# A gated mix of two spectral filters: frequency groups as the outer loop, rows turned from SBUF to SBUF, and one joint inverse

## Chip, cores, metric

One core of a Trainium2 chip. The metric is the device time of one execution in microseconds (us); results were compared with the reference. PE is TensorE, DVE is VectorE, ACT is ScalarE, POOL is GpSimd; SP is the engine that does nothing but issue DMAs here.

## The reference

```python
def _A_ref(x, w_r, w_i):                      # _B_ref is the same with B's filter
    X = jnp.fft.rfft2(x.astype(jnp.float32), axes=(-2, -1))   # x: 1 x 2048 x 1024
    X = X * (w_r + 1j * w_i)                                  # filter: 2048 x 513
    return jnp.fft.irfft2(X, s=(S, D), axes=(-2, -1)).astype(jnp.bfloat16)

g = sigmoid((A_x * gate_w).sum(-1, keepdims=True))            # one gate per row
return g * _A_ref(A_x, A_w_r, A_w_i) + (1 - g) * _B_ref(A_x, B_w_r, B_w_i)
```

The input is transformed once and multiplied by two filters of 2048 x 513 complex numbers; two inverse transforms are mixed by a gate for each row. Inputs and output are bf16, and the transforms are matrix products with fixed matrices: 2048 = 128 (n1) x 16 (n2) along the rows, 1024 along d with real and imaginary parts folded.

## The kernel before

It works on 16 groups `kg` of 128 row frequencies. `stage_d` transforms along d, `stage_s2` does the second step of the row transform, `prod` multiplies by a filter on DVE (two groups at once), and `stage_i1` starts the inverse with the *data* as the stationary matrix, so that its result comes out turned; the eviction scatters it with a stride of 128 elements. Then comes an inverse over d for each branch and each row group `n2`, and a last stage that mixes both branches.

```python
    def wload(b):                                  # a filter: 18 DMAs, mostly 256 rows of 1026 B each
        for pm in range(2):
            for ii in range(4):
                for c in range(2):
                    ...
                    if pm == 0:
                        part(16 * ii, 1, 0, 16)
                    elif ii < 3:
                        part(80 + 16 * ii, -1, 0, 16)
                    ...
        dma("sp", prs, [], [("W", b)] + ...)        # one event for the whole filter

    def stage_i1(b, kg):
        for lb in range(4):
            for c in range(2):
                w = ap(RING, p + c * 512 + lb % 2 * 256 + lb // 2, [[2, 128]])      # data is stationary
                fns.append(mm(pslot(s, lb * 256, [[1, 256]]), w, ap(KI, z + c * 256, [[1, 256]]), c == 0, c == 1))
        ...
        ev(1024, ap(VR[b], kg * 8, [[128, 128], [1, 8]]), pslot(s, 0, [[8, 128], [1, 8]]), [("ps", s)], w)

    def stage_dinv(b, n2):                         # inverse over d, once for each branch
        ...
    def s1inv(n2):                                 # n1 inverse, mixes A and B through RA and RB
        ...
    for t in range(16 + LAG):
        ...                                        # rest of stage_i1(1, .), gmix, stage_dinv(0, .)
    for t in range(17):
        if t < 16:
            stage_dinv(1, t)
        if t >= 1:
            s1inv(t - 1)
```

Of the kernel before, what the change touches and what calls it, by code (L numbers as in the profile page):

```python
# [4 lines left out]
dt = mybir.dt  # L5
ACT = mybir.ActivationFunctionType
ALU = mybir.AluOpType
AP = bass.AP
BF = dt.bfloat16

NS = 514
PW = 128
# [7 lines left out]

def make_consts():

# [5 lines left out]
    kord = (np.arange(16)[:, None] + 16 * np.arange(4)[None, :]).reshape(-1)  # L28
    k1 = kord[None, None, :]
# [5 lines left out]
    C["F"] = F.reshape(128, 2048)  # L35
# [5 lines left out]
    C["RM"] = R.reshape(128, 2048)  # L41
# [3 lines left out]
    for h in range(2):  # L45
        d = (h * 128 + np.arange(128))[:, None] + 0.5
        lev, lod = 2 * m, 2 * m + 1
        les = np.where(m == 0, 512, 2 * m)
        DM[:, 0, h] = np.cos(pi2 * lev * d / 1024)
        DM[:, 1, h] = -np.sin(pi2 * lod * d / 1024)  # L50
        DM[:, 2, h] = -np.sin(pi2 * les * d / 1024)
        DM[:, 3, h] = np.cos(pi2 * lod * d / 1024)
# [4 lines left out]
    for par in range(2):  # L57
        for h in range(2):
            l = (2 * (h * 128 + np.arange(128)) + par)[:, None]
            DI[:, par, h, 0] = np.where(l == 0, 1.0, 2.0) / 1024 * np.cos(pi2 * l * d / 1024)  # L60
            li = np.where(l == 0, 512, l)
            DI[:, par, h, 1] = -np.where(li == 512, 1.0, 2.0) / 1024 * np.sin(pi2 * li * d / 1024)
# [3 lines left out]
    KI = np.zeros((2, 2, 128, 2, 16, 4, 2))  # L66
    for z in range(2):
        for pm in range(2):
            for k2 in range(16):
                for ii in range(4):  # L70
                    i = ii if pm == 0 else 3 - ii
                    po = k2 * 8 + pm * 4 + ii
                    spec = (z == 1 and i == 0)
                    for q2 in range(16):
# [16 lines left out]
                        K = KI[z, :, po, :, q2, i, :]  # L91
# [11 lines left out]
    C["KI"] = KI.reshape(2, 2, 128, 256).transpose(2, 0, 1, 3).reshape(128, 1024)  # L103
    gs = np.full((64, 2), 8.0)
    gs[:, 1] = -8.0
    gs[0] = 4.0
    C["GS"] = np.repeat(gs.reshape(128, 1), 16, axis=1)
    one = np.zeros((128, 2))
    one[0] = 1.0
    C["ONE"] = one  # L110
    idt = np.zeros((128, 16))
    idt[:16] = np.eye(16)
    C["ID"] = idt
    return C


class Op:
    __slots__ = ("eng", "idx", "fns", "deps", "raw", "dma", "clock", "need", "count", "waits", "pos")

    def __init__(self, eng, idx, fns, dma, pos):  # L120
        self.eng, self.idx, self.fns, self.dma, self.pos = eng, idx, fns, dma, pos
        self.deps, self.raw = set(), set()
        self.need = False
        self.count = 0


class Sched:


    ENG = ("pe", "act", "dve", "pool", "sp")  # L130

    def __init__(self):
        self.q = {e: [] for e in self.ENG}
        self.all = []
        self.writer, self.readers = {}, {}

    def op(self, eng, fns, reads=(), writes=(), dma=False):
        if not isinstance(fns, (list, tuple)):
            fns = [fns]
        o = Op(eng, len(self.q[eng]), list(fns), dma, len(self.all))  # L140
        self.q[eng].append(o)
        self.all.append(o)
        for k in reads:
            assert k in self.writer, k
            o.deps |= self.writer[k]
            o.raw |= self.writer[k]
        for k in writes:
            o.deps |= self.writer.get(k, set())
            o.deps |= self.readers.get(k, set())
        for k in reads:  # L150
            self.readers.setdefault(k, set()).add(o)
        for k in writes:
            self.writer[k] = {o}
            self.readers[k] = set()
        o.deps.discard(o)
        return o

    def solve(self):
        known = {e: {} for e in self.ENG}

        def merge(kn, c):
            for k, v in c.items():
                if v > kn.get(k, -1):
                    kn[k] = v
        for o in self.all:
            kn = known[o.eng]
            o.waits = []
            for d in sorted(o.deps, key=lambda d: -d.pos):
                if d.dma:
                    if d in kn:  # L170
                        continue
                    kn[d] = 1
                else:
                    if d.eng == o.eng == "pe":
                        continue
                    if kn.get(d.eng, -1) >= d.idx:
                        continue
                    d.need = True
                o.waits.append(d)
                merge(kn, d.clock)  # L180
# [3 lines left out]
        for e in self.ENG:  # L184
# [5 lines left out]
    def emit(self, nc):  # L190
        self.solve()
        sems = {e: nc.alloc_semaphore("s_" + e) for e in self.ENG}
        dsem = {o: nc.alloc_semaphore(f"s_d{i}") for i, o in enumerate(o for o in self.all if o.dma)}

        def run(e, name):
            for o in self.q[name]:
                for d in o.waits:
                    if d.dma:
                        e.wait_ge(dsem[d], 16 * len(d.fns))
                    else:  # L200
                        e.wait_ge(sems[d.eng], d.count)
                for f in o.fns:
                    ins = f(e)
                    if o.dma:
                        ins.then_inc(dsem[o], 16)
                if o.need:
                    ins.then_inc(sems[name], 1)
            if name == "sp":
                for o in self.all:
                    if o.dma == "out":  # L210
                        e.wait_ge(dsem[o], 16 * len(o.fns))
# [22 lines left out]

def bass_gated_mix__spectral_gfnet__spectral_gfnet__prompt_kernel(
    nc, A_x, A_w_r, A_w_i, B_x, B_w_r, B_w_i, gate_w, out
):
    C = make_consts()
# [11 lines left out]
    R1 = sb("R1", 16384)  # L250
    R2 = sb("R2", 32 * NS)
    R3 = sb("R3", 16384)
    R4 = sb("R4", 16384)
    R5 = sb("R5", 32 * NS)
    FM = sb("FM", 2048)
# [3 lines left out]
    DI = sb("DI", 2048)  # L259
    RM = sb("RM", 2048)  # L260
    GS = sb("GS", 16)
    ONE = sb("ONE", 2)
    ID = sb("ID", 16)
    V6 = sb("V6", 256)
    RING = sb("RING", 11264)
    GROW = sb("GROW", 512)
    X5 = sb("X5", 32)
    P5 = sb("P5", 192)
    V5 = sb("V5", 256)
    ZG = sb("ZG", 16)  # L270
    G8 = sb("G8", 8)
# [3 lines left out]
    S = Sched()  # L275
# [4 lines left out]
    WR = {0: R5, 1: R2}  # L280


    load = {"act": 0.0, "dve": 0.0}
    slot_n = [0]
    nslots = [3]

    def slot():
        s = slot_n[0] % nslots[0]
        slot_n[0] += 1
        return s  # L290

    def dve(ns, fns, reads, writes):
        load["dve"] += ns
        return S.op("dve", fns, reads, writes)

    def ev(n, outap, inap, reads, writes, eng=None, bias=0.0):
        ca, cd = 170 + 0.833 * n, 150 + 1.04 * n
        if eng is None:
            eng = "act" if load["act"] + ca <= load["dve"] + cd + bias else "dve"
        load[eng] += ca if eng == "act" else cd  # L300
        if eng == "act":
            S.op("act", lambda e: e.activation(outap, inap, ACT.Copy), reads, writes)  # L302
        else:
            S.op("dve", lambda e: e.tensor_copy(outap, inap), reads, writes)  # L304

    def pslot(s, off, dims, p0=0, np_=128):
        return ap(PS, s * 1024 + off, dims, p0, np_)

    def misc(b, off, dims, np_=128):
        return ap(PS, b * 512 + off, dims, 0, np_)  # L310
# [7 lines left out]
    def dma(eng, pairs, reads, writes, kind=True):  # L318
        S.op(eng, [lambda e, d=d, s=s: e.dma_start(d, s) for d, s in pairs], reads, writes, dma=kind)  # L319

    def cload(eng, t, key, n):
        dma(eng, [(ap(t, 0, [[1, n]]).bitcast(dt.uint16), cst[key].ap())], [], [key])


    def xload(a, b):
        dma("sp", [(ap(R1, a * 1024, [[1024, b - a], [1, 1024]]), xv[:, a:b, :])], [], [("x", i) for i in range(a, b)])

    xload(0, 2)
    cload("sp", FM, "F", 2048)
    dma("act", [(ap(R2, 2048, [[1, 1024]], 0, 1), gate_w.rearrange("(o d) -> o d", o=1))], [], ["gw"])  # L330
    cload("act", ONE, "ONE", 2)
    for a, b in ((2, 4), (4, 8), (8, 12), (12, 16)):
        xload(a, b)
    cload("sp", DM, "DM", 2048)
    cload("sp", S2, "S2", 768)
    cload("sp", KI, "KI", 1024)
    cload("sp", GS, "GS", 16)
    cload("sp", ID, "ID", 16)

    def wload(b):  # L340

        prs = []
        T = WR[b]
        P = pit[id(T)]
        for pm in range(2):
            for ii in range(4):
                for c in range(2):
                    src = wsrc[b][c]
                    n = src.shape[-1]

                    def part(r0, step, k0, k1):
                        prs.append((AP(T, (4 * pm + ii) * P + (2 * k0 + c) * NS, [[8 * P, 16], [2 * NS, k1 - k0], [1, n]]),
                                    AP(src.tensor, src.offset + r0 * n, [[128 * n, 16], [step * n, k1 - k0], [1, n]])))
                    if pm == 0:
                        part(16 * ii, 1, 0, 16)
                    elif ii < 3:
                        part(80 + 16 * ii, -1, 0, 16)
                    else:
                        part(127, -1, 1, 16)
                        part(64, 1, 0, 1)  # L360
        dma("sp", prs, [], [("W", b)] + (["zrow", "gwt"] if b else []))
    wload(0)
# [283 lines left out]
```

## Time and profile before

| | before |
|---|---|
| time, median of 2 runs | 162.69 us (162.27 to 163.12) |
| span of the profiled execution | 159.0 us |
| mean granted clock of TensorE | 0.968 |
| busy: PE, DVE, ACT | 78%, 76%, 77% |
| last stage | 123 to 159, 36 us |

Two more views matter later. The first is the page's throughput line: 40 slices of the span, GB/s in each. The filters (8.4 MB) pass in slices 5 to 17 at about 170 GB/s, and then there is hardly any transfer until the output.

```profile
GB/s 168 296 429 415 257 168 167 177 167 165 179 168 170 181 169 169 197 191 4 0 0 0 0 5 0 0 0 4 0 0 1 4 112 152 86 180 123 145 132 132
```

The timeline of SP's queue gives start in us, duration, what is issued. SP issued these four filter loads after it had issued nothing for 1.7 us (32.45 to 34.19):

```profile
34.19 0.57 SPq L319 DMA_DIRECT2D R<-in_B_w_r_dram  x1
34.81 0.64 SPq L319 DMA_DIRECT2D R<-in_B_w_i_dram  x1
35.48 0.65 SPq L319 DMA_DIRECT2D R<-in_B_w_r_dram  x1
36.17 0.65 SPq L319 DMA_DIRECT2D R<-in_B_w_i_dram  x1
```

A filter load that nothing holds back keeps SP for about 0.6 us. Other issues of this kernel, of constants, show 0.42 to 0.58. Most of the filter loads of 256 KB show about 1.4 us, because there the DMA engines set the pace; so the 0.6 us of the issue itself cost nothing here.

### The profile page before, as it was taken

Reading aid. Unit: us, or ns where it says so; the run is one execution under the profiler, and the core shown is the slowest. Engines: PE = TensorE matmul, PEld = TensorE weight load, DVE = VectorE, ACT = ScalarE, POOL = GpSimd, SP = SyncE. Lnnn points to the kernel's source line nnn. Section 1 sums busy time; section 2 is a strip of 40 time slices with the busy share of each in tenths; the row PEclk is TensorE's granted clock in tenths of the full one; section 3 lists DMA queues with packets and bytes.
Section 4 is the critical chain, followed back from the end, with each engine's and each line's share of the span. In section 5 each row is a group of like instructions: output and inputs, shape, how many; then the busy total and the mean of one; then the engine's idle time right before and its main releaser. Section 6 shows DMA issues by size and latency. Waiting matters only on the chain.

```text
span 159.0 us, 2541 instructions
## 1 busy us (share of the span) xinstructions
PE 124.6 (78%) x1015; PEld 90.0 (57%) x1024; DVE 120.4 (76%) x193; ACT 121.7 (77%) x132; POOL 0.2 (0%) x4
## 2 busy tenths in 40 slices
PE   0255897888928999999954999959999899898930
PEld 0244654355616767776633788847778576565600
DVE  0699998000079997998999999969923788989892
ACT  3045889629985988989955599999999499888850
POOL 0000000000000000000000000000000000000000
PEclk9999999999999999999995599999999999999995
DMA  5899999999999999950000000000000034243333
GB/s 168 296 429 415 257 168 167 177 167 165 179 168 170 181 169 169 197 191 4 0 0 0 0 5 0 0 0 4 0 0 1 4 112 152 86 180 123 145 132 132
DMA packets 13165, 19.53 MB, mean 123 GB/s; under 512 B 1505, under 2 KB 9825, under 8 KB 12770
## 3 DMA queue, kind: packets, MB, share of 16 engines
q1 hardware_dynamic: 13008, 19.37, 53.5%
q8 instruction: 8, 0.13, 0.4%
q14 instruction: 3, 0.02, 0.1%
q10 hardware_dynamic: 146, 0.00, 0.0%
HBM read 15.17 MB, written 4.19 MB: 122 GB/s over the span
## 4 chain that ended last, share of the span: by engine, by line
ACT 37%; PE 27%; DVE 22%; issue 7%; DMA 4%; SPq 1%; DVEq 0%
PE PS L313 27%; ACT R L302 21%; ACT RING L302 13%; DVE RING L316 12%; DVE R L316 6%; DMA R<-in_A_x_dram 4%; DVE RING L304 4%; ACT GROW L564 1%; ACT L564 1%; ACT V L302 1%; SPq L319 1%; DVEq L213 0%
## 5 line engine op out<-in xcount | busy, mean ns | idle before, releaser
L302 ACT ACTIVATE R<-PS 128x1024 bf16<-128x1024 f32 (+1 forms) x80 | 75.9, 1041 | 20.9 <-PE PS L313 20.9
L316 DVE TENSOR_TENSOR RING<-R 128x2048 bf16<-128x2048 bf16 (+1 forms) x48 | 48.0, 1041 | 16.9 <-DMA R<-in_A_w_i_dram 10.2
L302 ACT ACTIVATE RING<-PS 128x1024 bf16<-128x1024 f32 x40 | 42.8, 1135 | 8.0 <-PE PS L313 6.8
L316 DVE TENSOR_TENSOR RING<-RING 128x512 bf16<-128x512 bf16 (+1 forms) x96 | 44.6, 509 | 2.5 <-ACT RING L302 1.4
L313 PE MATMUL PS<-KI,RING 128*128 128x256 bf16 x256 | 34.0, 281 | 7.5 <-issue 3.1
L313 PE MATMUL PS<-DI,R 128*128 128x256 bf16 x256 | 32.7, 273 | 1.5 <-DVE RING L304 1.2
L313 PEld LDWEIGHTS PS<-KI,RING 128*128 128x128 bf16 x256 | 24.3, 101 | 14.0 <-issue 3.9
L313 PEld LDWEIGHTS PS<-DI,R 128*128 128x128 bf16 x256 | 24.4, 98 | 8.4 <-DVE RING L304 2.2
L313 PE MATMUL PS<-FM,R 128*128 128x128 bf16 x128 | 11.8, 266 | 13.0 <-DVE R L316 13.0
L313 PEld LDWEIGHTS PS<-FM,R 128*128 128x128 bf16 x128 | 10.1, 122 | 14.8 <-DVE R L316 14.4
L313 PE MATMUL PS<-RING,S 128*128 128x1 bf16 (+2 forms) x91 | 15.8, 304 | 1.3 <-ACT RING L302 1.1
L313 PE MATMUL PS<-DM,R 128*128 128x256 bf16 x128 | 16.4, 273 | 0.2 <-DVE RING L304 0.2
L313 PEld LDWEIGHTS PS<-DM,R 128*128 128x128 bf16 x128 | 12.0, 98 | 2.5 <-DVE RING L304 0.5
L313 PEld LDWEIGHTS PS<-RING,S 128*128 128x128 bf16 x96 | 7.8, 97 | 7.7 <-ACT RING L302 1.4
L304 DVE CAST RING<-PS 128x1024 bf16<-128x1024 f32 x8 | 10.0, 1251 | 1.9 <-PE PS L313 1.9
L316 DVE TENSOR_TENSOR R<-RING 128x1024 bf16<-128x1024 bf16 x16 | 10.3, 688 | 0.3
L313 PE MATMUL PS<-R,FM 128*128 128x512 bf16 x30 | 9.1, 379 | 1.3 <-DVE RING L304 1.3
L313 PE MATMUL PS<-RING,DM 128*128 128x512 bf16 x30 | 9.1, 379 | 0.1
L313 PE MATMUL PS<-R,G 128*1 128x512 bf16 x32 | 7.5, 378 | 0.7 <-ACT R L302 0.7
L304 DVE CAST R<-PS 128x1024 bf16<-128x1024 f32 x4 | 4.9, 1223 | 3.1 <-PE PS L313 3.1
L316 DVE TENSOR_TENSOR ZG<-PS,GS 128x16 bf16<-128x16 f32 x1 | 0.2, 175 | 6.8 <-PE PS L313 6.8
L313 PEld LDWEIGHTS PS<-RING,DM 128*128 128x128 bf16 x32 | 3.1, 98 | 3.8
(25 smaller groups left out, 26.9 us busy)
## 6 DMA issues: line engine op xcount, KB each, us to landing
out_dram<-RING SPq DMA_DIRECT2D x16, 256.0 KB, 2.0
R<-in_A_x_dram SPq DMA_DIRECT2D x3, 1024.0 KB, 10.5
R<-in_A_w_r_dram SPq DMA_DIRECT2D x7, 256.5 KB, 13.9
R<-in_A_w_i_dram SPq DMA_DIRECT2D x7, 256.5 KB, 14.7
R<-in_B_w_r_dram SPq DMA_DIRECT2D x7, 256.5 KB, 14.4
R<-in_B_w_i_dram SPq DMA_DIRECT2D x7, 256.5 KB, 14.1
R<-in_A_x_dram SPq DMA_DIRECT2D x2, 512.0 KB, 5.0
FM<-c_F SPq DMA_DIRECT2D x1, 512.0 KB, 5.0
```

What stands on the lines that cost most here:

```text
L302: S.op("act", lambda e: e.activation(outap, inap, ACT.Copy), reads, writes)
L304: S.op("dve", lambda e: e.tensor_copy(outap, inap), reads, writes)
L313: return lambda e: e.matmul(o, l, r, start=start, stop=stop, skip_group_check=True)
L316: return lambda e: e.tensor_tensor(out=o, in0=a, in1=b, op=op)
L319: S.op(eng, [lambda e, d=d, s=s: e.dma_start(d, s) for d, s in pairs], reads, writes, dma=kind)
L564: S.op("act", lambda e: e.activation(ap(GROW, 0, [[1, 512]]), misc(7, 0, [[1, 512]]), ACT.Sigmoid), ["m7"], ["GROW"])
```

## The change

The intent: carry each frequency group through products and both first inverses while later ones are still in the forward part; take `KI` as the stationary matrix, so that evictions are contiguous; let DMA turn the rows from SBUF to SBUF (the *turns*), as DMA was idle there; mix the branches in the n1 inverse, so that only one inverse over d is needed; and fix the order of all instructions on each engine by a small model that runs when the kernel is built. So that products can start before the filters are whole, these come in three chunks of frequency groups: 0 to 2, 2 to 8, 8 to 16. That makes 36 + 32 + 32 = 100 DMAs out of 36.

```diff
+WCH = ((0, 2), (2, 8), (8, 16))
+WPRIO = (-85, -83, 34)
 ...
+    def dma(name, pairs, deps=(), prio=0.0, size=0.0, eng="sp", kind="in", use=(), n=1, sem=None):
+        P.add(name, {eng: 0.5 * n}, ...)          # the model: 0.5 us of SP for each issue
+    def wload(b, k0, k1, prio):
+        for c in range(2):
+            for ii in range(4):
+                for pm in range(2):
+                    ...                            # 16 x (k1 - k0) rows of 1026 B
+            if k0 == 0:
+                ...                                # 64 rows more
+        n = 18 if k0 == 0 else 16
+        for i in range(0, n, 2):
+            dma(f"W{b}.{k0}.{i}", lambda i=i: pairs()[i:i + 2], ...)
 ...
     def stage_i1(b, kg):
-                w = ap(RING, p + c * 512 + lb % 2 * 256 + lb // 2, [[2, 128]])
-                fns.append(mm(pslot(s, lb * 256, [[1, 256]]), w, ap(KI, z + c * 256, [[1, 256]]), c == 0, c == 1))
-        ev(1024, ap(VR[b], kg * 8, [[128, 128], [1, 8]]), pslot(s, 0, [[8, 128], [1, 8]]), [("ps", s)], w)
+        for lc in range(2):
+            for c in range(2):
+                fns.append(mm(ap(PS, bb[lc] * 512, [[1, 512]]), ap(KI, z + (lc * 2 + c) * 128, [[1, 128]]),
+                              ap(W, p0 + c * 514 + lc, [[1, 512]]), c == 0, c == 1))
+        P.add(f"T.{b}.{kg}", EV, ...)              # contiguous eviction
+        def turn():                                # 128 partitions to 8: row group n2 into the free dimension
+            return [(AP(U, dp_of(kg, 0) * q + b * 1024, [[4 * q, 8], [2048, 16], [1, 1024]]), ap(W, t0, [[1, 1024]]))]
+        dma(f"U.{b}.{kg}", turn, [f"T.{b}.{kg}"] + alln1, t + PR["turn"], 1.25, kind="turn")
 ...
-    def stage_dinv(b, n2): ...      def s1inv(n2): ...
+    for n2 in range(16):
+        P.add(f"n1i.{n2}", ...)     # 16 matmuls of 128 columns, both branches; waits for all 32 turns
+        P.add(f"y.{n2}", EV, ...)   # eviction
+        P.add(f"di.{n2}", ...)      # one inverse over d, 8 matmuls of 256 columns
+        P.add(f"o.{n2}", EV, ...)   # eviction, then four DVE operations and the output DMA
+    order = P.run()                 # the model decides order, engine and buffers (PSUM bank pairs too)
```

The forward part changes too: one of DVE's two folding passes goes into TensorE by a doubled matrix F, and the gate row is computed later.

## The prediction

> **What bounds the kernel now.** I read the page first (busy times and slices), then a table of stages, then the DMA issues in time, then groups by shape. The page names no single bound:
>
> ```profile
> PE 124.6 (78%) x1015; PEld 90.0 (57%) x1024; DVE 120.4 (76%) x193; ACT 121.7 (77%) x132; POOL 0.2 (0%) x4
> ...
> PEclk9999999999999999999995599999999999999995
> DMA  5899999999999999950000000000000034243333
> ```
>
> Three engines share the work evenly, and DMA is full for the first 44% of the span and nearly empty after that. So the bound changes along the way. The table of stages, cut where the work changes (columns: PE, weight loads, DVE, ACT, POOL, clock, DMA share, GB/s), shows how:
>
> ```profile
> 0.00:34.00 34.00, 19.67 (x183) 13.11 (x184) 21.57 (x36) 18.99 (x22) 0.20 (x4) 1.00 1.00 254
> 34.00:44.50 10.50, 9.40 (x79) 6.47 (x78) 0.17 (x1) 9.32 (x9) 0.00 (x0) 1.00 1.14 170
> 44.50:71.00 26.50, 23.10 (x188) 16.94 (x189) 25.12 (x27) 21.41 (x22) 0.00 (x0) 1.00 1.06 182
> 71.00:123.00 52.00, 45.19 (x397) 36.00 (x396) 43.69 (x61) 46.20 (x54) 0.00 (x0) 0.93 0.00 1
> 123.00:159.00 36.00, 27.23 (x181) 17.45 (x182) 29.82 (x69) 25.77 (x28) 0.00 (x0) 0.95 0.32 118
> ```
>
> Forward transforms and gate to 34; then DVE does nothing for 10 us because the first filter (W of A) has not landed; from 44.5 to 123 all three engines are busy, with almost no DMA after 71; then the last stage, 36 us for 16 row groups. The idle line in the timeline:
>
> ```profile
> 44.59 2.36 DVE L316 TENSOR_TENSOR RING<-R 128x2048 bf16<-128x2048 bf16 x2 [10.21 <-DMA R<-in_A_w_i_dram]
> ```
>
> The durations I use below (mean ns last before the bar):
>
> ```profile
> L302 ACT ACTIVATE R<-PS 128x1024 bf16<-128x1024 f32 x76 | 73.6, 1065 | 17.9 <-PE PS L313 17.9
> L316 DVE TENSOR_TENSOR RING<-R 128x2048 bf16<-128x2048 bf16 x32 | 37.7, 1219 | 11.3 <-DMA R<-in_A_w_i_dram 10.2 <-ACT R L302 1.0
> L316 DVE TENSOR_TENSOR RING<-RING 128x1024 bf16<-128x1024 bf16 x32 | 20.6, 684 | 0.2 <-PE PS L313 0.2
> ```
>
> and the filter loads as SP issues them (256.5 KB each, 256 rows of 1026 B), plus the small ones:
>
> ```profile
> 20.91 1.41 SPq L319 DMA_DIRECT2D R<-in_A_w_r_dram  x1
> 22.36 1.44 SPq L319 DMA_DIRECT2D R<-in_A_w_i_dram  x1
> ...
> out_dram<-RING SPq DMA_DIRECT2D x16, 256.0 KB, 2.0
> ```
>
> An issue by itself takes 0.33 to 0.68 us; here it takes 1.4, so the queues are full and the engines pace it: 1.42 us for 16 rows per DMA engine, 89 ns a row. All 8.4 MB of filters need about 32 x 1.42 = 45 us by this, and took from 17 to 71 us.
>
> **What the skill says.** "DMA: Bandwidth & Descriptors", section "Why a DMA increments its semaphore by 16 and not by 1": the number of DMA engines is the largest k up to 16 that divides the slowest dimension of both sides, and HWDGE takes the lowest-numbered k. The new SBUF-to-SBUF turn has 128 partitions on the source and 8 on the destination, so all 32 turns go to the same 8 engines. No transfer of the kernel before has such a shape, so its trace cannot confirm this. The same page, "Why small descriptors are slow (HBM only)", puts a cost on small HBM descriptors; the trace agrees in kind: 1 KB rows run at 170 GB/s, the 4 to 8 KB rows of x reach 429. "TensorE: Matmul & The Clock Gate", section "Back-to-back issue gap", gives about 81 ns per 128-column matmul with its weight load; here 16 such pairs occupy 0.90 us of weight loads at full clock, 56 ns each, so I use 56. The same page's cold state (half clock after some us of idle) agrees with the two 5s in the PEclk line.
>
> **The change part by part.**
>
> Front. The second fold goes into TensorE (except for two of 16), so DVE's two passes per row pair (4 x 0.68 = 2.7 us) become one (1.37): 11 us less. The gate row moves off the path (from 27 to 34 us it stood alone on it), another 5 to 6. x and the doubled matrix F are 5 MB; the slices moved that much by about 16 us. The last rows then need a fold (1.5), matmuls (0.9) and an eviction: Z is whole at about 22 us instead of 34. First product: d, Q, s2, X follow one another, 0.9 + 1.2 + 0.95 + 1.0, so 26 us instead of 44.6, if W is there.
>
> Middle. Per frequency group PE needs d 0.87, s2 0.92, two inverses of 4 x 512 columns 1.76: 3.55 us. ACT: Q, X and two T at about 1.05: 4.2. DVE for two branches: 2 x (2 x 0.61 + 2 x 0.34) = 3.8. Over 16 groups ACT and DVE each have some 63 to 66 us (the four single groups cost more, three evictions go to DVE). Unhindered, products would end at 26 + 66 = 92, and the last turn would land near 97. The rival on DMA decides whether that holds.
>
> DMA. After 17.5 us of x, F and constants, SP issues 36 small filter loads of 16 to 64 rows (1 MB in all). At about 0.45 us each, by the issues above, they end near 26 us and carry 6 us of work: some 6 us of idle DMA. Then comes the rest: the filters as a whole 42 to 46 us, 32 turns, and RM and DI 2.6. A turn is 128 pieces of 2 KB on 8 engines, 16 each. The output's 2 KB packets take 87 ns in the packet records, so 1.2 to 1.4 us a turn, 39 to 45 for 32. All but two turns are queued behind the last filter chunk. Sum on the lower 8 engines: 17.5 + 6 + 44 + 41.5 (32 x 1.3) + 2.6 = 111.6, less the couple of us in which parts of the first chunk go under the x load: about 110. The second half of B's filter lands near 68 to 72, while DVE wants it at about 71, so DVE loses 5 to 8 us in waits for chunks (B's first, A's and B's second, B's third), and products end near 99. That is still before the turns: the middle ends at 110, not 97.
>
> End. Per row group n2: PE 16 x 56 ns + 0.87 = 1.77 us; ACT two evictions, 1.95; DVE four 512-column operations, 1.55. ACT bounds it at 16 x 1.95 = 31.2, since all 32 evictions are placed on ACT. Head 1.5 (a cold PE adds some), tail of DVE and output 4.5 (the kernel before has 3.1 from its last DVE operation group to the end): 37.5, against 36 before. The joint inverse saves 16 evictions overall, but they were in the middle, before 123.
>
> Sum: 110 + 37.5 = 147.5 span, plus the 3.7 by which the measured time exceeds the span now: **151 us**, 7% faster.
>
> **Rivals.** (1) *Turns never bind*: pieces overlap on an engine, or a turn uses all 16. Then the end starts at about 99 + 5 = 104, and with no filter waits at 97: 138 to 145 us. For: the writer's own layout puts the eight destination partitions apart. Against: 8 in the destination shape. (2) *DMA is worse than I have it*: filter rows at 97 ns (170 GB/s) instead of 89 and turns at 1.4 or above: the end starts at 118 to 120, time 160, within 2%. For: that was the average over 34 to 44.5. Against: consecutive loads now alternate between the two halves of the partitions, which may help. (3) *ACT binds the middle*: Q's eviction now reads PSUM in two interleaved streams; at 1.35 (as the strided-write form cost before) ACT has 70 us and the middle ends at 98: hidden below the turns. (4) *Static order stalls*: the order is fixed from a model; a late filter chunk stops DVE, then ACT and PE through X and Q buffers. I have 5 to 8 us for this; another 5 would still hide below 110.
>
> **Range and chances.** Rival 1 gives 138 to 145, the centre 151, rival 2 160. I hold 142 to 161 for 8 in 10. Faster by over 2% means under 159.4: 0.80; within 2%: 0.14; slower: 0.06.
>
> **What would show it.** In the profile after: first product at 26 us; DVE waits on W DMAs of a few us each; DMA full until about 110 with GB/s falling when only turns run; a turn taking 8 engines; PE waiting on a turn DMA for 5 to 12 us before the last stage, with a clock dip; a last stage of about 37 us with ACT over 85% busy. If the last stage starts at 97 or PE's last wait is on ACT or DVE, the DMA step was wrong; if products start after 35, the front was.

## The result, and the profile after

Ratios in this document are the mean time of one kernel's runs over the mean of the other's runs of the same rounds, so not quite the ratio of the medians that are quoted. Executions over 1.5% slower than the fastest of the same kernel are left out of the means.

| | before | after |
|---|---|---|
| time, median | 162.69 us | 168.82 us (168.70 to 168.94) |
| ratio | | 1.039 (1.028 to 1.050) |
| span, mean clock | 159.0 us, 0.968 | 166.9 us, 0.890 |
| busy us: PE, DVE, ACT | 124.6, 120.4, 121.7 | 122.0, 110.6, 107.0 |
| last stage starts, takes | 123, 36 us | 124.5, 42.4 us |

Slower by 3.9%, although the engines have less to do: DVE 10 us less, ACT 15. The page after (busy times, then 40 slices: clock, DMA share, GB/s):

```profile
PE 122.0 (73%) x923; PEld 75.6 (45%) x930; DVE 110.6 (66%) x183; ACT 107.0 (64%) x120; POOL 0.7 (0%) x6
...
PEclk9869999999985899999999999755555899999997
DMA  5899932146565588677558655555520023333333
GB/s 131 269 407 427 351 63 51 36 114 158 151 152 146 145 216 232 167 210 201 153 201 256 243 204 204 201 202 201 201 101 4 12 115 128 126 126 130 127 126 126
```

Before, DMA was full until the filters were in. Here it falls to 36 to 63 GB/s in slices 5 to 7 and stays near 150 for six more, at half share or so, *while filters are still wanted*. Slices 14 to 28 pass 153 to 256 GB/s; in the last six of them, when only turns run, it is 201 to 204 at a share of 0.5, as if half of the DMA engines were full and the other half idle (turn16 below tests this). The clock line falls to 0.5 in slices 26 to 30, around PE's long wait, and is still low when PE works again at 124.5.

The table of stages (columns: PE, weight loads, DVE, ACT, POOL, clock, DMA share, GB/s):

```profile
0.00:29.00 29.00, 23.04 (x178) 16.48 (x180) 15.81 (x29) 18.86 (x21) 0.67 (x6) 0.94 0.74 244
29.00:54.00 25.00, 16.20 (x96) 7.71 (x96) 15.35 (x23) 12.68 (x16) 0.00 (x0) 0.89 0.50 125
54.00:79.00 25.00, 24.24 (x149) 11.53 (x145) 22.02 (x23) 19.88 (x24) 0.00 (x0) 0.98 0.73 195
79.00:112.00 33.00, 23.28 (x123) 10.51 (x124) 31.73 (x44) 23.36 (x28) 0.00 (x0) 0.92 0.58 208
112.00:124.50 12.50, 1.67 (x4) 0.30 (x2) 1.35 (x3) 1.02 (x1) 0.00 (x0) 0.50 0.47 178
124.50:131.00 6.50, 6.46 (x57) 5.87 (x58) 0.06 (x1) 3.08 (x3) 0.00 (x0) 0.55 0.01 3
131.00:163.00 32.00, 27.15 (x329) 23.18 (x328) 22.96 (x61) 28.11 (x29) 0.00 (x0) 1.00 0.30 116
```

The first product comes at 29.3 instead of 44.6: that gain is real. From 29 to 54 DVE works 15 of 25 us. Its longer waits there and just after are for filter chunks (2.7 and 3.3 us) and for an X (4.3 us), while DMA is half empty: the bytes it waits for could have been moved. From 79 to 112 DVE is full. From 112 to 124.5 hardly any engine works (PE 1.7 of 12.5 us); DMA does. SP's queue shows why:

```profile
9.04 5.74 SPq L428 DMA_DIRECT2D W<-in_A_w_r_dram  x9
...
26.91 5.67 SPq L428 DMA_DIRECT2D W<-in_B_w_i_dram  x9
...
48.89 5.45 SPq L428 DMA_DIRECT2D W<-in_B_w_i_dram  x8
54.39 1.46 SPq L428 DMA_DIRECT2D U<-W  x2
...
73.14 5.10 SPq L428 DMA_DIRECT2D W<-in_B_w_i_dram  x8
78.29 8.78 SPq L428 DMA_DIRECT2D U<-W  x8
...
90.42 24.96 SPq L428 DMA_DIRECT2D U<-W  x21
```

The nine smallest loads (16 to 64 rows) take 5.7 us, 0.64 from one start to the next (0.60 of it the issue itself), the eight of 128 rows at the end 5.10, also 0.64: the issue of a filter load costs the same, however many rows it moves. SP issues filters from 9.04 to 78.29 with hardly a break. The first chunk's 36 loads take it 23.6 us and carry 1.05 MB (45 GB/s), the second's 32 take 21.8 us and carry 3.15 MB (145 GB/s), the third's 32 take 22.4 us and carry 4.2 MB (188 GB/s); before, filters passed at 170 to 182. All three chunks go at the pace of the issuer: in the third, too, all but two of the 32 issues take 0.60 us, and the DMA share from 56 to 78.3 is 0.74. That its rate equals the one before is chance. In the packet records a row of 1026 B takes 107 ns on average before and 62 ns here (8192 such packets in each run); why they are faster was not examined.

SP works through its queue in order, so 30 of the 32 turns stand behind the last filter load, whatever time their rows were ready. From 90 on SP takes 1.19 us for each turn: there the engines hold it back. The last eviction for a turn ends at 114.7, the last turn lands ten microseconds later. PE then waits (wait in brackets), and the loop of the last stage runs as in these lines:

```profile
124.54 3.60 PE L412 MATMUL PS<-Z,U 128*128 128x128 bf16 x32 [10.87 <-DMA U<-W]
```

```profile
133.12 1.05 PE L412 MATMUL PS<-Z,W 128*128 128x256 bf16 x8 [0.22 <-ACT W L419]
134.01 1.06 PE L412 MATMUL PS<-Z,U 128*128 128x128 bf16 x16
134.21 1.94 ACT L419 ACTIVATE W<-PS 128x1024 bf16<-128x1024 f32 x2 [0.23 <-PE PS L412]
135.28 1.05 PE L412 MATMUL PS<-Z,W 128*128 128x256 bf16 x8 [0.22 <-ACT W L419]
```

A period is 135.28 - 133.12 = 2.16 us. An inverse over d (`Z,W`) runs from 133.12 to 134.17; ACT begins to evict it at 134.21, needs a little over 1 us, and only then, at 135.28, may the next inverse start. So inverse and eviction form a chain of 1.05 + 1.03 us and two hand-overs, which is the period. The plan that the kernel makes when it is built gives 15 of these 16 inverses the same pair of PSUM banks, 0 and 1; the last one gets 2 and 3.

Two causes are suspected: **the issue of filters** on SP (and with it the turns that queue behind), and **the bank pair** in the last stage. A rival for the first: the turns on 8 engines alone, so that the backlog would be there anyway; another: small filter pieces move slowly on the DMA engines.

### The profile page after: what moved, and what is told of

Its sections match the earlier page's. It is cut to its first block, busy times and chain, and to the rows that moved or that the text cites. A ratio compares the mean times of both kernels' runs of the same rounds, so it can differ in the third digit from the quotient of the medians.

```text
span 166.9 us, 2467 instructions
## 1 busy us (share of the span) xinstructions
PE 122.0 (73%) x923; PEld 75.6 (45%) x930; DVE 110.6 (66%) x183; ACT 107.0 (64%) x120; POOL 0.7 (0%) x6
## 4 chain that ended last, share of the span: by engine, by line
DVE 30%; SPq 29%; PE 15%; ACT 11%; DMA 7%; issue 5%; DVEq 0%
SPq L428 29%; DVE FM L415 18%; PE PS L412 15%; DVE W L415 12%; ACT W L419 11%; DMA U<-W 6%; DMA W<-in_B_w_i_dram 1%; DVEq L328 0%; DVE XR L420 0%; DVE ZG L415 0%
## 5 line engine op out<-in xcount | busy, mean ns | idle before, releaser
L419 ACT ACTIVATE W<-PS 128x1024 bf16<-128x1024 f32 x63 | 62.4, 1043 | 30.0 <-PE PS L412 30.0
L415 DVE TENSOR_TENSOR FM<-XR,W 128x2056 bf16<-128x2056 bf16 (+1 forms) x40 | 40.6, 1016 | 11.6 <-DMA W<-in_B_w_i_dram 6.0
L412 PE MATMUL PS<-W,KI 128*128 128x512 bf16 x124 | 34.0, 409 | 17.0 <-DVE W L415 13.7
L415 DVE TENSOR_TENSOR W<-W 128x512 bf16<-128x512 bf16 x64 | 24.4, 422 | 26.6 <-ACT W L419 26.0
L412 PE MATMUL PS<-Z,U 128*128 128x128 bf16 x256 | 18.7, 233 | 10.9 <-DMA U<-W 10.9
L415 DVE TENSOR_TENSOR W<-FM 128x1028 bf16<-128x1028 bf16 (+1 forms) x40 | 23.5, 588 | 1.4
L412 PEld LDWEIGHTS PS<-Z,U 128*128 128x128 bf16 x256 | 17.4, 106 | 12.2 <-DMA U<-W 11.8
L412 PE MATMUL PS<-Z,W 128*128 128x256 bf16 x128 | 17.5, 283 | 2.9 <-ACT W L419 2.9
L419 ACT ACTIVATE QR<-PS 128x1024 bf16<-128x1024 f32 x16 | 16.3, 1075 | 1.9 <-PE PS L412 1.9
L412 PE MATMUL PS<-QR,S 128*128 128x512 bf16 (+2 forms) x93 | 15.9, 305 | 0.8 <-DVE FM L415 0.6
L419 ACT ACTIVATE ZR<-PS 128x512 bf16<-128x512 f32 x1 | 0.6, 597 | 13.1 <-PE PS L412 13.1
```

Source lines behind the costliest of these rows:

```text
L412: return lambda e: e.matmul(o, l, r, start=start, stop=stop, skip_group_check=True)
L415: return lambda e: e.tensor_tensor(out=o, in0=a, in1=b, op=op)
L419: return lambda e: e.activation(o, i, ACT.Copy)
```

## The experiments

All runs are compared with the kernel before on the same chip. The before medians of the three groups were 160.73, 160.97 and 162.53 us. Results were correct unless said otherwise. The changed kernel was not run beside the first two groups, so a comparison with it goes by ratios, or by stages within the traces, where chips can differ by about 1%.

### First group: move or widen one thing each

**w_pool**: the 50 issues of B's filter go to GpSimd. One line where instructions are put into queues:

```diff
+        q = "pool" if t.name.startswith("W1.") else t.on
-        o = S.op(t.on, fns, set(), t.kind, t.sem)
+        o = S.op(q, fns, set(), t.kind, t.sem)
```

> Same instruction order on PE, ACT, DVE; the 50 filter loads of B are issued by GpSimd in place of SP. Theory 1 (SP's 0.60 to 0.64 us per issue, 100 filter issues from 9 to 78 us, holds back the filters and the turns queued behind them): the filters are in at 64 to 70 us in place of 79, DVE's wait for B before 56 us shrinks and products end at 101 to 104 in place of 110, the last turn lands at 110 to 115 in place of 124.5; time 155 to 160 us. Rival A (the DMA engines' own rate for 1 KB rows holds them, as in the kernel before): filters still end after 76 us, time within 3 us of 168.8. Rival B (GpSimd issues slower than SP): B lands later than now, time above 170.

Measured: 165.15 us, ratio 1.027 (1.022 to 1.032). Against the changed kernel's 1.039 that is a gain of a little over 1%, within the latter's interval, and not what the issue theory expected (155 to 160 us). DVE's timeline tells why; its first product:

```profile
41.58 1.43 DVE L415 TENSOR_TENSOR FM<-XR,W 128x1028 bf16<-128x1028 bf16 x2 [4.46 <-DMA W<-in_A_w_i_dram]
```

At 41.6 instead of 29.3. GpSimd had nothing to hold it back and started on B's filter at 1.5 us, beside x: DVE's waits for x rose from 6.7 to 13.1 us, and the first product then waited another 4.5 us for A's filter. After that, DVE worked from 41.6 to 113.9 almost without a wait. The experiment had moved two things at once, the issuer and the order, and could not tell them apart; hence w_gate below.

**turns_pool**: the turns, not the filters, go to GpSimd (`startswith("U.")` in the same place).

> Same order on PE, ACT, DVE; all 32 turns issued by GpSimd, so that they do not stand behind the filter loads in SP's queue. Theory 1 and 2 (turns wait for SP's filter issues, then drain at 1.3 us each on 8 engines): turns run from about 33 us on, beside the filters; the last lands 3 to 6 us after its T eviction at 114.8, the last stage starts at 118 to 120; time 162 to 164. If turns slow the filters by sharing engines, products end later than 110 by 2 to 5 us and the gain shrinks to nothing. Rival (turns do not set the start of the last stage): PE still waits till 124 and time stays 168.8.

Measured: 176.74 us, ratio 1.098 (1.093 to 1.103). The expectation was wrong in sign. With a queue of their own the turns no longer stand behind the filters, and then the last filter chunk is slower: SP's last 16 filter issues take 1.04 us each instead of 0.69. That the turns compete with them for the DMA engines is the likely reading. DVE's timeline:

```profile
96.56 2.49 DVE L415 TENSOR_TENSOR FM<-XR,W 128x2056 bf16<-128x2056 bf16 x2 [12.98 <-DMA W<-in_B_w_i_dram]
```

Products stop for 13 us for the last filter chunk, and the last stage starts at 133.55. A turn is of no use before the last stage; a filter is wanted at once. That the turns stood *behind* filters was no fault as such.

**turn16**: wrong (relative error 1.4): a turn writes the same bytes to 128 partitions instead of 8.

```diff
-            return [(AP(U, dp_of(kg, 0) * q + b * 1024, [[4 * q, 8], [2048, 16], [1, 1024]]), ap(W, t0, [[1, 1024]]))]
+            return [(ap(U, (b * 16 + kg) * 1024, [[1, 1024]]), ap(W, t0, [[1, 1024]]))]
```

> Wrong result on purpose: the turns write 128 partitions x 2 KB straight in place of 8 partitions x 16 pieces; same bytes, same pieces of 2 KB, same issues and order. Theory 2 (a turn runs on 8 of 16 DMA engines, so 30 turns take about 40 us): on 16 engines a turn takes about 0.7 us, the backlog at 114 us is gone, the last stage starts at 117 to 119; time 161 to 163, and GB/s in the stretch with turns alone is issue-paced or near 400 when backlogged. Rival (1.3 us per turn comes from SP's issue or from 2 KB pieces from SBUF to SBUF, not from the number of engines): GB/s stays 200 and time 168 to 169.

Measured: 160.72 us, ratio 1.002 (0.995 to 1.008). The same stretch in the table of stages, turn16 and then the changed kernel:

```profile
79.00:100.00 21.00, 17.62 (x110) 9.19 (x110) 20.38 (x23) 19.57 (x25) 0.00 (x0) 1.00 0.87 314
```

```profile
79.00:100.00 21.00, 16.76 (x102) 8.58 (x102) 20.35 (x24) 16.82 (x22) 0.00 (x0) 1.00 0.61 211
```

314 GB/s against 211: the shape of the destination does confine a turn to half of the engines. PE's wait before the last stage falls from 10.9 to 3.4 us, and that stage starts at 117.4. By the ratios the 8 engines cost about 6 us in this state, by the spans (166.9 and 158.7, of two chips) 8. That is not yet a cause: it may be a cost only because the turns start late (last group).

**ps_alt**: `pick`, which gives out PSUM banks, gives every second inverse over d the pair 6; the built plan then has pair 0 once, and after that 6 and 2 in turn.

```diff
-        for b in free:
-            if b % 2 == 0 and b + 1 in free:
+        for b in ((6 if int(key[3:]) % 2 else 0, 0, 2, 4, 6) if key.startswith("di.") else free):
+            if b % 2 == 0 and b in free and b + 1 in free:
```

> Only the PSUM banks of the 16 last inverses over d change: they alternate between pairs in place of all using banks 0 and 1. Theory 3 (in the last stage the next inverse waits for the eviction of the one before from the same banks, a loop of 1.06 + 1.03 + 0.07 = 2.16 us): the period falls to ACT's 1.95 and the last stage is 3 us shorter; time 165 to 166. Rival (ACT's two evictions or the PE clock set the period): period stays 2.16, time 168.8.

Measured: 163.62 us, ratio 1.019 (1.016 to 1.021). The start of the last stage stays at 124.8, its length falls from 42.4 to 36.9 us, the period from 2.16 to 1.84. ACT's timeline in it:

```profile
129.28 16.60 ACT L419 ACTIVATE W<-PS 128x1024 bf16<-128x1024 f32 x18
```

18 evictions without a gap, 0.92 us each. In the stage the gain is larger than the 3 us expected (5.5); by the ratios it is 3.3. The order on every engine is the one of the changed kernel, only the banks differ, so this cause is shown: the stage is now bound by ACT, as the prediction had it.

### Second group: the issue apart from the order

**w_gate**: w_pool, with GpSimd's first filter load waiting for the last of x.

```diff
+        if t.name == "W1.0.0":
+            o.deps.add(ops["x12"])
```

> As the run with B's filters on GpSimd (ratio 1.027), but GpSimd's first filter load waits until the last x rows have landed, so that filters do not overtake x (there the first product came at 41.6 us in place of 29.3; DVE then ran without filter waits for 72 us). Theory 1: first product at 29 to 31 us, no filter wait over 3 us on DVE, products end at 101 to 104, turns are backlogged at 1.3 us each on 8 engines until 110 to 113; ratio to the kernel before 0.95 to 0.98. Rival (filters arrive no faster however they are issued): DVE still waits 6 us or more for B, products end after 108; ratio above 1.02.

Measured: 152.76 us, ratio 0.952 (0.948 to 0.957). GpSimd's issues start at 18.14 and take about 0.52 us each; DVE's longest wait in the middle is no longer for a filter:

```profile
18.14 4.65 POOL L428 DMA_DIRECT2D W<-in_B_w_r_dram  x9 [16.95 <-DMA U<-in_A_x_dram]
```

```profile
59.18 2.49 DVE L415 TENSOR_TENSOR FM<-XR,W 128x2056 bf16<-128x2056 bf16 x2 [1.62 <-ACT XR L419]
```

All filters are issued by 53, products end at 101.8 (110.6 in the changed kernel), the last stage starts at 109.0, where the prediction had 110. Bytes and turns are the same as in the changed kernel. Three things differ: half of the filters have another issuer, A's later chunks no longer stand behind B's, and the packets of B's filter are larger. The pages of the changed kernel and of w_gate:

```profile
DMA packets 19293, 28.43 MB, mean 170 GB/s; under 512 B 2513, under 2 KB 11345, under 8 KB 19154
```

```profile
DMA packets 16509, 28.43 MB, mean 189 GB/s; under 512 B 2513, under 2 KB 7377, under 8 KB 16370
```

SP's loads are packets of one row (1026 B); of GpSimd's, 384 have two rows, 800 have four and only 128 have one. So w_gate shows what a second issuer brings, but not the issue's time alone; w_few and w_more do that better. It does show that the engines could take more: SP issued A's first 34 loads about every 0.67 us, nearly as before, GpSimd another every 0.52 beside them, and DMA moved 234 GB/s from 18.1 to 53.

**w_few**: the issuer stays SP, and the number of issues falls from 100 to 68: the first two chunks become one.

```diff
-WCH = ((0, 2), (2, 8), (8, 16))
-WPRIO = (-85, -83, 34)
+WCH = ((0, 8), (8, 16))
+WPRIO = (-85, 34)
```

> All on SP as in the change; only the first two filter chunks are merged: 68 filter issues in place of 100 for the same bytes (the order of products stays, a few evictions move). Theory 1 (SP's time per issue, near 0.6 us whatever the size): the issues end some 19 us earlier, near 59 to 64 us, then limited by the DMA engines' rate; DVE's first wait for B grows (B's merged chunk lands at 40 to 44), later waits vanish; products end at 106 to 110; the last turn lands at 110 to 114; ratio 0.96 to 1.00. Rival (bytes, not issues, set when the filters are in): filters in at 76 us or later, ratio 1.03 or above.

Measured: 155.05 us, ratio 0.964 (0.958 to 0.969). SP's queue and PE's timeline:

```profile
53.12 6.18 SPq L428 DMA_DIRECT2D W<-in_B_w_i_dram  x8
...
60.45 46.76 SPq L428 DMA_DIRECT2D U<-W  x31
```

```profile
110.65 3.52 PE L412 MATMUL PS<-Z,U 128*128 128x128 bf16 x32 [5.14 <-DMA U<-W]
```

Filters are issued by 59.3 instead of 78.3, that is 19.0 us sooner with 32 issues fewer; turns go from 60.5 on, still at about 200 GB/s, and PE waits 5.1 us for the last one instead of 10.9. Products end at 102.9. This is the cleanest evidence that the number of issues on one queue set the time: the same bytes in the same packets (8192 rows of 1026 B) in fewer DMAs. Not quite all else is equal: A's groups 2 to 8 now come before B's first, and the model moved seven evictions to another engine and shifted the order of work in places.

**w_gate_ps**: w_gate and ps_alt together.

> The run above with the alternating PSUM banks of the last stage. If the two costs are separate, it is 3 to 3.5 us below the run above (the banks alone brought 3.3 us); ratio 0.93 to 0.96. If the last stage after an earlier start has another bound, under 1.5 us.

Measured: 148.30 us, ratio 0.925 (0.920 to 0.931): the best correct kernel. The last stage starts at 108.4 and takes 36.7 us. The gain over w_gate is 4.5 us by the medians, more than the 3 to 3.5 expected; the two causes add up, as they should if they are two.

**w_gate_ps_turns**: the same with the turns on GpSimd too.

> The run above with all turns on GpSimd as well, behind B's filters. Theory 2 (turns on the lower 8 engines are the last wait): if GpSimd's turns spread over both halves of the engines, the backlog goes and the last stage starts 4 to 6 us after the last eviction of T, another 2 to 4 us less; ratio 0.91 to 0.94. Rival (GpSimd's turns stay on 8 engines, or each turn costs it more than 1.5 us to issue): no gain or a loss against the run above.

Measured: 150.50 us, ratio 0.938 (0.932 to 0.943): 1.3% slower than with the turns on SP. DVE waits 3.7 us for A's last chunk, and the last stage starts at 113.2. The rival of the expectation came out; it is turns_pool again, in small.

### Third group: the other direction, and what is left of the 8 engines

**after_again**: the changed kernel, unaltered, for this group's chip.

> The changed kernel as it is, beside the others of this call, for a closer ratio and for the spread from chip to chip. Every theory: 1.03 to 1.05.

Measured: 168.86 us, ratio 1.042 (1.032 to 1.051), in agreement with the first result. The last stage starts at 126.2 here, 1.7 us later than in the first trace.

**w_more**: the middle chunk cut in two: 132 issues.

```diff
-WCH = ((0, 2), (2, 8), (8, 16))
+WCH = ((0, 2), (2, 5), (5, 8), (8, 16))
```

> Opposite of the merged chunks: the second filter chunk is cut in two, so 132 filter issues on SP in place of 100, same bytes. Theory 1 (0.60 to 0.64 us per issue, filters then turns behind them): filter issues end 16 to 20 us later, at 94 to 98, the last turn lands at 136 to 142, the last stage starts there; ratio 1.11 to 1.15. Rival (issues hide behind the data): ratio 1.03 to 1.06.

Measured: 188.90 us, ratio 1.167 (1.156 to 1.178), somewhat beyond what was expected. SP's queue and the page's throughput:

```profile
93.49 5.10 SPq L428 DMA_DIRECT2D W<-in_B_w_i_dram  x8
98.63 8.96 SPq L428 DMA_DIRECT2D U<-W  x8
```

```profile
GB/s 140 297 409 415 188 42 46 62 81 75 77 74 80 83 64 78 112 227 221 204 205 163 196 249 223 204 203 201 201 201 146 4 56 112 116 116 141 140 112 112
```

The last filter load is issued at 98.6 instead of 78.3: 20.3 us for 32 issues more, 0.64 each. Over eleven slices DMA moves 42 to 83 GB/s of the same filters that passed at 170 before the change. The last stage starts at 144.8, 20.3 us later than in the first trace of the changed kernel (18.6 later than in after_again). The rival that small pieces are slow on the DMA engines is out: wherever SP issues all filters, the kernel before included, every piece is a row of 1026 B, and the DMA share of those slices is 0.2 to 0.3. Nor do the loads queue up there: the median load of 48 KB lands 2.2 us after its issue.

**w_few_ps**: w_few and ps_alt, with nothing on GpSimd.

> Merged chunks on SP and the alternating PSUM banks, nothing on GpSimd. If both add up (0.9635 and 3.3 to 5 us): ratio 0.930 to 0.945. If the banks bring nothing here: 0.96.

Measured: 150.48 us, ratio 0.927 (0.918 to 0.936). Its last stage starts at 111.3. That is the time of w_gate_ps within the noise, with one issuer and no GpSimd. Two tuples and a rule in `pick` turn a loss of 4% into a gain of 7%.

**w_gate_ps_16**: wrong: the best kernel with turn16's turns.

> Wrong result on purpose: the best version (ratio 0.925) with turns written straight to 128 partitions, on 16 engines. Theory: the 8 engines cost 8 us in the change only because the turns started late; where filters are in at 50 us, turns keep up and only the last one's time counts: under 2 us gain, ratio 0.910 to 0.925. Rival (8 engines cost as much whenever turns are used): 6 us or more, ratio under 0.89.

Measured: 147.41 us, ratio 0.908 (0.899 to 0.917). The span of its profiled run is 145.7 us, that of w_gate_ps 145.1. With filters in early, 16 engines bring 0.6% by the medians, 1.9% by the ratios (these are of two chips, whose before runs differ by 1%) and nothing in the spans, against some 3.6% in turn16 (1.002 over 1.039). The start of the last stage, in w_gate_ps and then here, moves by 0.4 us, where turn16 moved it by 7.1:

```profile
108.42 3.36 PE L412 MATMUL PS<-Z,U 128*128 128x128 bf16 x32 [5.15 <-DMA U<-W]
```

```profile
108.01 3.60 PE L412 MATMUL PS<-Z,U 128*128 128x128 bf16 x32 [3.39 <-DMA U<-W]
```

So the 8 engines were costly in the changed kernel mainly *because* the turns started at 78.

## Why the prediction was wrong, point by point

Predicted 151, measured 168.8. The span was to be 147.5 and is 166.9, that is 19.4 us more: the last stage starts 14.5 us late (124.5 for 110) and takes 4.9 us longer (42.4 for 37.5). Against that stands 1.8 us: the time exceeds the span by 1.9 now, not by 3.7. (The 3.7 was the time of some runs less the span of another run; where the record has both of one run of the kernel before, the difference is 1.5 to 1.6. So this term, too large by about 2 us, hid a part of the miss.) 19.4 - 1.8 = 17.6, and 0.2 had been rounded off the prediction: 17.8, the miss.

**The step that failed** is the price of the filter loads: "At about 0.45 us each, by the issues above, they end near 26 us and carry 6 us of work: some 6 us of idle DMA. Then comes the rest", and this rest was priced by bytes alone. The first 36 loads took 0.64 us each and ended at 32.6: **6.6 us**. The second chunk took 21.8 us of issues for 3072 rows, by the prediction's bytes (1.42 us for 256 rows) 17.0: **4.8 us** more. The third took 22.4 us, by bytes 22.7; this agreement is luck, as SP set the pace there too and the engines had become faster for each row. In the sum that led to 110, everything before the turns was 17.5 + 6 + 44 = 67.5; measured, the filters were through at about 79, and of these 11.5 us the two terms make 11.4. The turns with RM and DI were to take 41.5 + 2.6 = 44.1 and took 124.5 - 79 = 45.5 (two had gone before): 1.4. And the 1.6 us taken off for filter pieces under the x load did not come. Together 14.5. What the runs showed in its place is a path of 100 issues on SP at 0.64 us, with the turns behind them: w_few took 32 issues away and gained 19.0 us in the filters' end, w_more added 32 and lost 20.3; w_gate supports it from another side.

The number that would have prevented it stood in the trace before: the four filter loads quoted above, 0.57 to 0.65 us each when nothing held them back. The prediction gave the right range for an issue by itself (0.33 to 0.68), and then took a value from its lower part, where x, constants and output stand. With 0.65, the 36 small loads after 9.0 us end at 32.4; the trace has 32.6. The kernel's own model has the same fault with its 0.5 us.

**The second step**: "ACT bounds it at 16 x 1.95 = 31.2 ... 37.5". It holds only where the inverses over d have two bank pairs: with ps_alt the stage took 36.9. The changed kernel ran at 2.16 us a period, as each inverse waited for the eviction of the one before. Of the 4.9 us by which the stage was longer, 16 x (2.16 - 1.95) = 3.4 are this. The rest lies in head and tail, which took 42.4 - 16 x 2.16 = 7.8 us for the 6.0 predicted (PE's clock was 0.55 until 131); the prediction's terms, 31.2 + 1.5 + 4.5, add up to 37.2, not 37.5. And 36.9 in ps_alt is close in part by luck: a period was 1.84 there, not 1.95, with a longer head and tail. The wait for the banks was not among the rivals, and was to be seen before the run: the order and the buffers are fixed when the kernel is built.

**What held.** The turns run on half of the engines, as the rule that the prediction takes from the Trainium skill has it (201 GB/s at a share of 0.5, and 314 GB/s at 0.87 in turn16; which 8 was not looked at), and take 1.30 us (262,144 B at 201 GB/s), against 1.2 to 1.4; PE waits for a turn before the last stage, with a clock dip. It is 10.9 us, within the 5 to 12, but the prediction had it on top of products that end at 99, not at 110.6. DVE's work for a group, two branches, was 3.98 us with gaps, against 3.8. The front came 3 us late (first product at 29.3, not 26). Evictions took 1.04 to 1.08 us, so the rival on Q was out. Other agreements are luck. w_gate's last stage starts at 109.0, near the predicted 110, and the spans of w_few_ps and w_gate_ps, 149.3 and 145.1, lie near 147.5, but by another path: in w_gate the filters are issued by 53, not through at 67.5, the turns are not backlogged, and the last stage starts 4.1 us after the last eviction for a turn, as in the prediction's first rival; its products just end later (101.8) than the 99 given there, and the way from products to the last stage is 7.2 us, not 5.

**The rivals.** "DMA is worse than I have it" named the right place and the wrong reason: rows and turns at the engines' rate, not the issuer. "Static order stalls" was part of it: the waits for chunks (2.7 and 3.3 us) are within the 5 to 8, but DVE also waited 4.3 us for an X, and with some 71 us of work and small gaps (for 66) after 29.3 it came to 110.6. The larger part of the slow filters showed in no wait of DVE at all, but as turns that queued.

**Left open.** Why an issue of these loads costs SP 0.60 us, while one of an output store (256 KB) costs 0.33 in the same trace; number of dimensions, shape and address pattern were not varied. Why a row of 1026 B took 107 ns before and 62 ns after. Why turns issued from GpSimd cost more than from SP: order and engine may both play a part.

## What to carry to other kernels

Count the DMA issues of each queue as you count instructions of an engine: issues times the duration of *the same kind of issue* in a trace, and set it beside the time of the bytes; whichever is larger is the load time. Cutting a transfer into chunks to start earlier is worth it only as long as the chunk's bytes take longer than its issue, and whatever stands behind it in the same queue pays too. Put in order what is wanted first (filters before turns, x before filters), and look at which buffers a planner hands out: one pair of banks in a loop can undo the overlap it planned.

## What the Trainium skill lacked or had wrong

- "DMA: Bandwidth & Descriptors", section "Issuing engines are not separate DMA queues": issuing from several engines only saves the issuer's time, "which is usually small relative to the DMA itself". Here that time was the limit: 0.64 us on SP for a load of 16 to 128 rows of 1026 B, a hundred times, 69 us from first to last; with 32 issues fewer the ratio went from 1.039 to 0.964, with half of them on GpSimd (0.52 us each) and in the right order to 0.952. The page has no time of an issue from SP measured on this chip, and does not say that it depends on the transfer: in the changed kernel 0.33 for an output store, 0.43 to 0.65 for constants and F ahead of the filters, 0.60 for a filter load.
- The same page, section "Rules for kernel authors", says to coalesce many small transfers and that under 64 KB one pays mostly overhead. The runs agree and put the border higher where one queue issues everything: loads of 98 KB (96 rows) passed at 145 GB/s and those of 131 KB at 188, both at the issuer's pace.
- "TensorE: Matmul & The Clock Gate", section "Back-to-back issue gap", has about 81 ns for a matmul of 128 columns with its weight load. In ps_alt 16 such pairs of the last stage begin 0.89 us before the group that follows them without a wait, 56 ns each, as the prediction had taken from the trace of before.
